# Rewriting the first batch of a fused attention and mixer kernel: casts and squares on another engine, the first rsqrt earlier, and a later mixing schedule

## Chip, cores, metric

The kernel runs on one core of one Trainium2 chip. The metric is device microseconds of one execution; lower is better. Most numbers below are medians of several executions. "Granted clock" is the share of the full TensorE clock that the chip allowed on average over an execution.

## The reference

Eight batches of 12 heads, 448 positions and head width 64 go through attention with RMS-normalised queries and keys, and then through a mixer: a rank-32 mix over positions, and a two-layer network over 768 channels with 3072 hidden ones.

```python
q_n, k_n = rmsnorm(q, g_q), rmsnorm(k, g_k)        # x / sqrt(mean(x*x) + 1e-6) * g
attn = softmax(q_n @ k_n.T / sqrt(64)) @ v         # per head
x = attn with heads side by side                   # (8, 448, 768)
u = x + (x.T @ U @ V).T                            # U: 448 x 32, V: 32 x 448
out = u + relu(u @ w_ch1) @ w_ch2                  # 768 -> 3072 -> 768
```

## The kernel before

The program is recorded in a fixed order, and each engine is given its own instructions in that order; the timelines below show them starting in it. In steady state the attention of the next batch is woven into the two-layer network of the current one. Batch 0 has nothing to be woven into: its attention runs alone, and this part (the "head", about 46 us) is what the change rewrites.

A group ("t") is 4 heads; a pair ("p") is 2 heads, so batch 0 has groups 0 to 2 and pairs 0 to 5. Each pair has four exponentials of 112 x 896, so the head has 24 "slots", numbered 0 to 23. In each slot one exponential is issued on ScalarE, then the pieces listed for that slot, then the score multiply of two slots later.

```python
def squares(t, hs=ALL, ss=(0, 1), eng=None):      # s=0: keys, s=1: queries
    ...
        if (t < 2 or t > 5) and eng is None:
            nc.scalar.activation(sqs[t, s][:, hs], qks[t, s][:, hs], AF.Square)
        else:
            nc.gpsimd.tensor_tensor(sqs[t, s][:, hs], qks[t, s][:, hs], qks[t, s][:, hs], OP.mult)
def reduce(t, hs, ss): ...       # VectorE: sums of the squares -> rstd
def rsqrt(t, hs): ...            # ScalarE: Ln, then Exp(-0.5 x), on rstd
def scale(t, pr): ...            # VectorE: qkn = qk * rstd, two tensor_tensor with two SBUF inputs
def transposes(p): ...           # TensorE, then two VectorE copies into qkT
def yield_port(t, pr):           # GpSimd waits here until that scale is done
    nc.gpsimd.tensor_copy(scratch, qkns[2 * t + pr][0:1, 1, 0, 0, 0:1])
def values(p, hh): ...           # TensorE: o = E^T va; VectorE: reciprocal, x, xs
def mix_a(b, dc): ...            # TensorE: pm = x_cols * U; VectorE: t4b <- pm
def mix_b(b, dc):                # TensorE: pu = t4b * V + x_cols
    ...
        if dc in (0, 5):
            nc.scalar.activation(us[b][:, dc, :], pu, AF.Copy)
        else:
            nc.vector.tensor_copy(us[b][:, dc, :], pu)
def heat(n): ...                 # n filler multiplies of 128 x 512, meant to keep TensorE's clock up
def first(i, dcs, start): ...    # first-layer multiplies of hidden blocks 2i and 2i+1
```

The order of the head, cut to what is argued about:

```python
heat(NWARM)                                  # NWARM = 16
squares(0, A); reduce(0, A)                  # A: first two heads of group 0, Bh: the others
nc.vector.tensor_mul(grow[:, 0], grow[:, 0], grow[:, 1])
squares(0, Bh, (0,)); rsqrt(0, A); squares(0, Bh, (1,))
reduce(0, Bh, (0,)); scale(0, 0); gain(); reduce(0, Bh, (1,))
transposes(0); heat(3)
squares(1, ALL, (0,), nc.gpsimd)
rsqrt(0, Bh)
scores(0, (0, 1))
at(0, scale, 0, 1)  ...  at(0, transposes, 1)
at(1, squares, 1, ALL, (1,))  ...  at(1, squares, 2)          # the first on ScalarE, the second on GpSimd
at(3, rsqrt, 1); at(3, scale, 1, 0)  ...
at(5, transposes, 2); at(5, scale, 1, 1)  ...
at(11, setup_v); at(11, rsqrt, 2); at(11, scale, 2, 0)
at(12, mix_a, 0, 0)
...
at(22, values, 4, 1); at(22, mix_a, 0, 3)
at(23, mix_b, 0, 3);  at(23, mix_a, 0, 4)
# after slot 23
first(0, range(0, 3), True)
values(5, 0); values(5, 1); mix_b(0, 4)
first(0, (3,), False); first(1, range(0, 4), True)
mix_a(0, 5); first(0, (4,), False); first(1, (4,), False); mix_b(0, 5)
...
```

The softmax here doesn't subtract the row's maximum and nothing guards it: scores larger than these inputs give would overflow.

Of the kernel before, what the change touches and what calls it, by code (L numbers as in the profile page):

```python
# [12 lines left out]
AF = mybir.ActivationFunctionType  # L13
# [4 lines left out]
def kernel(  # L18
# [13 lines left out]
    nc = tc.nc  # L32
# [7 lines left out]
    NJ = 4  # L40
# [43 lines left out]
    V4 = consts.tile([P, S], BF16, name="V4")  # L84
# [2 lines left out]
    grow = consts.tile([1, 2, 2, D], FP32, name="grow")  # L87
    one = consts.tile([1, 1], FP32, name="one")
    eps = consts.tile([SP, 1], FP32, name="eps")
    NWARM, NH = 16, 2  # L90
    FA, FM, NPE, FA0 = (0.74, 0.77), 0.09, 14, 0.66
    flat = Tw.rearrange("p f c n -> p (f c n)")
    lent = [0]
# [43 lines left out]
    def gain():  # L137

        pg = ps_mm.tile([P, 1], FP32, tag="mm")
        nc.tensor.matmul(pg, grow[:, 0].rearrange("o a d -> o (a d)"), one, start=True, stop=True)  # L140
        nc.vector.tensor_copy(gg, pg)
# [4 lines left out]
    Vf = lend(P, [S], FP32)  # L146
# [5 lines left out]
        nc.sync.dma_start(Vf, moe_V.rearrange("r s -> () r s").to_broadcast([4, rank, S]))  # L152

    def setup_v():
        nc.scalar.activation(V4.rearrange("r (j p) -> r j p", j=NJ), Vf.rearrange("r (p j) -> r j p", j=NJ), AF.Copy)
        nc.gpsimd.tensor_copy(Vsh[:, 0, 0:64], V4[:, 384:448])
        nc.gpsimd.tensor_copy(Vsh[:, 1, 64:128], V4[:, 0:64])

# [56 lines left out]
    ALL = slice(0, HG)  # L215

    def squares(t, hs=ALL, ss=(0, 1), eng=None):
        for s in ss:
            if (t, s) not in sqs:

                sqs[t, s] = early[0:SP, t, s] if t < 4 else norm.tile([SP, HG, NJ * D], FP32, tag="sq", name="sq", bufs=1)
# [5 lines that stand above are left out]
    def reduce(t, hs=ALL, ss=(0, 1)):  # L227
        if t not in rstds:
            rstds[t] = norm.tile([SP, 2, HG, NJ], FP32, tag="rstd", name="rstd", bufs=3)
        for s in ss:  # L230
            nc.vector.tensor_reduce(rstds[t][:, s, hs].rearrange("p h j -> p (h j)"),  # L231
                                    sqs[t, s][:, hs].rearrange("p h (j d) -> p (h j) d", d=D), AX, OP.add)

    def rsqrt(t, hs=ALL):
        rs = rstds[t][:, :, hs].rearrange("p s h j -> p s (h j)")
        nc.scalar.activation(rs, rs, AF.Ln, bias=eps)
        nc.scalar.activation(rs, rs, AF.Exp, scale=-0.5)  # L237

    def scale(t, pr):
        rstd, qkn = rstds[t], norm.tile([SP, 2, NJ, 2, D], BF16, tag="qkn", name="qkn")  # L240
        qkns[2 * t + pr] = qkn
        hp = slice(2 * pr, 2 * pr + 2)
        for s in range(2):
            nc.vector.tensor_tensor(  # L244
                qkn[:, s].rearrange("p j h d -> p h j d"),
                qks[t, s][:, hp].rearrange("p h (j d) -> p h j d", d=D),
                rstd[:, s, hp].rearrange("p h j -> p h j ()").to_broadcast([SP, 2, NJ, D]),
                OP.mult)

    def transposes(p):  # L250
        qkn = qkns[p].rearrange("p s j h d -> p (s j) (h d)")
        qkT = attn.tile([P, 2, S], BF16, tag="qkT")
        qkTs[p] = qkT
        if p < NPE:
            pt = ps_mm.tile([P, 2, S], BF16, tag="mm")
            for i in range(2 * NJ):
                nc.tensor.transpose(pt.rearrange("d s (j p) -> d (s j) p", j=NJ)[:, i, :], qkn[:, i, :], ident[:SP, :SP])
            nc.vector.tensor_scalar(qkT[:, 1], pt[:, 1], gg, None, OP.mult)
            nc.vector.tensor_copy(qkT[:, 0], pt[:, 0])
        else:  # L260
            nc.sync.dma_start_transpose(qkT.rearrange("d s (j p) -> d (s j) p", j=NJ), qkn)

# [97 lines left out]
    def mix_b(b, dc):  # L360

        xt, cs = x_tiles(b), slice(dc * P, (dc + 1) * P)
        pu = ps_mm.tile([P, 384], FP32, tag="mm")
        nc.tensor.matmul(pu, t4s[b][:, cs], V4[:, 0:384], start=True, stop=False)
        for i in range(3):
            nc.tensor.matmul(pu[:, i * P:(i + 1) * P], xt[i][:, cs], ident, start=False, stop=(i == 2))
        if dc in (0, 5):
            nc.scalar.activation(us[b][:, dc, :], pu, AF.Copy)
        else:
            nc.vector.tensor_copy(us[b][:, dc, :], pu)  # L370
# [145 lines left out]
    def attention(b, extra={}):  # L516
# [14 lines left out]
        for p in range(b * 6, b * 6 + 6):  # L531
# [32 lines left out]
            if p + 1 < NPE and odd:  # L564
                add(.5, transposes, p + 1)
# [25 lines left out]
    def head():  # L591

        A, Bh = slice(0, 2), slice(2, 4)
        load(0, 2)
        load(1)
        load(2)
        load_mix()
        load_v(0)
        load_v(1)
        load_v(2)  # L600
        load(3)
        load_v(3)
        setup()
        heat(NWARM)
        squares(0, A)
        reduce(0, A)
        nc.vector.tensor_mul(grow[:, 0], grow[:, 0], grow[:, 1])
        squares(0, Bh, (0,))
        rsqrt(0, A)
        squares(0, Bh, (1,))  # L610
        reduce(0, Bh, (0,))
        scale(0, 0)
        gain()
        reduce(0, Bh, (1,))
        transposes(0)
        heat(3)
        squares(1, ALL, (0,), nc.gpsimd)
        rsqrt(0, Bh)
        scores(0, (0, 1))
        fill = {n: [] for n in range(24)}  # L620

        def at(n, fn, *args):
            fill[n].append(lambda: fn(*args))

        at(0, scale, 0, 1)
        at(0, reduce, 1, ALL, (0,))
        at(0, heat, 3)
        at(0, transposes, 1)
        at(1, heat, 3)
        at(1, squares, 1, ALL, (1,))  # L630
        at(1, reduce, 1, ALL, (1,))
        at(1, yield_port, 0, 1)
        at(1, squares, 2)
        at(1, load_w1, 0)
        at(2, heat, 2)
        at(3, rsqrt, 1)
        at(3, scale, 1, 0)
        at(3, yield_port, 1, 0)
        at(3, nc.gpsimd.tensor_copy, Uc, Uf)
        at(3, cast_v, 0)  # L640
        at(3, heat, NH)
        at(4, heat, 2)
        at(5, heat, 1)
        at(6, heat, 1)
        at(5, transposes, 2)
        at(5, scale, 1, 1)
        at(5, yield_port, 1, 1)
        at(6, cast_v, 1)
        at(6, load_w1, 1)
        at(7, setup_u, 0)  # L650
        at(7, reduce, 2, ALL, (0,))
        at(8, transposes, 3)
        at(8, reduce, 2, ALL, (1,))
        at(8, cast_v, 2)
        at(9, setup_u, 1)
        at(9, heat, 1)
        at(10, values, 0, 0)
        at(11, values, 0, 1)
        at(11, setup_v)
        at(11, rsqrt, 2)  # L660
        at(11, scale, 2, 0)
        at(12, mix_a, 0, 0)
        at(12, heat, 1)
        at(13, transposes, 4)
        at(13, scale, 2, 1)
        at(13, load, 4)
        at(13, load_v, 4)
        at(13, load_w1, 2)
        at(14, values, 1, 0)
        at(14, yield_port, 2, 1)  # L670
        at(14, squares, 3)
        at(15, values, 1, 1)
        at(16, transposes, 5)
        at(16, load, 5)
        at(16, load_v, 5)
        at(16, load_w1, 3)
        at(16, cast_v, 3)
        at(16, mix_b, 0, 0)
        at(17, values, 2, 0)
        at(18, values, 2, 1)  # L680
        at(18, mix_a, 0, 1)
        at(19, values, 3, 0)
        at(19, mix_b, 0, 1)
        at(20, values, 3, 1)
        at(20, mix_a, 0, 2)
        at(21, values, 4, 0)
        at(21, mix_b, 0, 2)
        at(22, values, 4, 1)
        at(22, mix_a, 0, 3)
        at(23, mix_b, 0, 3)  # L690
        at(23, mix_a, 0, 4)
        for n in range(24):
            expo(*divmod(n, 4))
            for piece in fill[n]:
                piece()
            if n + 2 < 24:
                scores((n + 2) // 4, ((n + 2) % 4,))
        first(0, range(0, 3), True)
        values(5, 0)
        values(5, 1)  # L700
        mix_b(0, 4)
        first(0, (3,), False)
        first(1, range(0, 4), True)
        mix_a(0, 5)
        first(0, (4,), False)
        first(1, (4,), False)
        mix_b(0, 5)
        reduce(3)
        rsqrt(3)
        first(0, (5,), False)  # L710
        first(1, (5,), False)
        scale(3, 0)
        scale(3, 1)
        squares(4, ALL, (0,))
# [40 lines left out]
    def heat(n):  # L755
        if n:
            warm = ps_mm.tile([P, 512], FP32, tag="mm")
            for _ in range(n):
                nc.tensor.matmul(warm, xss[1][:, 0:P], xss[1][:, 0:512], start=True, stop=True)  # L759
# [46 lines left out]
```

## Time and profile before

| | before |
|---|---|
| median of the first 3 executions | 580.83 us (579.06 to 581.6) |
| median with 3 more, taken beside the changed kernel | 579.7 us (578.13 to 581.6) |
| profiled execution | 578.24 us, span 576.5 us, granted clock 1.0 |

From the page of the profile of before: the first line is the span, then each engine's busy time with its share of the span, then TensorE's busy tenths and its granted clock in 40 equal slices.

```profile
span 576.5 us, 11342 instructions
PE 559.5 (97%) x4590; PEld 305.9 (53%) x4613; DVE 395.5 (69%) x811; ACT 280.1 (49%) x413; POOL 77.4 (13%) x122
PE   7899999999999999999999999999999999999997
PEclk9999999999999999999999999999999999999999
```

TensorE (PE) is busy 97% of the span. Only 17 us are not, and over half of them lie in the first 46 us. The next view is busy time by stretch of the same execution; the columns are the stretch, its length, the busy time and count of TensorE, weight loads, VectorE, ScalarE and GpSimd, then the granted clock, the DMA share and GB/s.

```profile
0.00:11.68 11.68, 7.51 (x33) 2.98 (x33) 5.32 (x11) 4.69 (x9) 5.82 (x22) 1.00 0.81 198
11.68:28.50 16.82, 14.20 (x146) 7.08 (x147) 15.32 (x30) 16.13 (x22) 10.78 (x15) 1.00 1.14 233
28.50:37.73 9.23, 8.58 (x158) 6.08 (x156) 7.44 (x31) 7.42 (x9) 5.43 (x6) 1.00 1.16 244
37.73:45.60 7.87, 6.65 (x77) 4.35 (x77) 5.27 (x15) 0.49 (x1) 2.98 (x3) 1.00 1.12 236
100.00:576.00 476.00, 469.22 (x3659) 253.85 (x3678) 316.70 (x632) 219.17 (x323) 37.75 (x62) 1.00 0.42 96
```

From 11.68 to 28.5 us ScalarE is busy 16.1 of 16.8 us and VectorE 15.3: these two pace the front. From 28.5 us on TensorE paces, and after 100 us it has almost no gaps. Here is the timeline of ScalarE in the front (start, length, engine, line, operation, tiles; in brackets the idle time before it and what ended it):

```profile
6.73 0.63 ACT L223 ACTIVATE w2b<-qk 112x512 f32<-112x512 f32 x1 [1.47 <-DMA qk<-in_k_dram]
7.26 0.29 ACT L236 ACTIVATE rstd<-rstd,eps 112x16 f32<-112x16 f32 x1
...
10.60 0.31 ACT L236 ACTIVATE rstd<-rstd,eps 112x16 f32<-112x16 f32 x1 [2.21 <-DVE rstd L231]
...
11.68 1.73 ACT L278 ACTIVATE E<-sc 112x896 bf16<-112x896 f32 x2 [0.53 <-PE sc L273]
13.29 1.06 ACT L223 ACTIVATE w2b<-Tw 112x1024 f32<-112x1024 f32 x1
14.24 1.73 ACT L278 ACTIVATE E<-sc 112x896 bf16<-112x896 f32 x2
15.83 0.34 ACT L236 ACTIVATE rstd<-rstd,eps 112x32 f32<-112x32 f32 x1
```

The first rsqrt (7.26 us) stands behind squares that wait for a load, although its sum was ready at about 6.0 us. The "end of the head" is here and below the first multiply of tile `ph`, where the rest of the first layer begins; 24 multiplies of that layer are done earlier by `first`, among the mixing, from 38.98 us on. Between the last exponential (36.80 us) and the end of the head (45.60 us) TensorE has two waits:

```profile
engine line waited for: us in total, times, longest us
PE pu L364 <- DVE t4b L358: 0.8, 1, 0.8
PE first L732 <- ACT u L368: 0.6, 1, 0.6
```

The 0.8 us is `mix_b(0, 3)` in slot 23: it waits for the VectorE copy of `mix_a(0, 3)` issued just before it.

### The profile page before, as it was taken

The page shows a single profiled execution, that of the slowest core. Times are in us where ns is not written, and L with a number is a line of the kernel's source. Part 1 is how long each engine was busy: PE and PEld are TensorE (multiplying, and loading weights), DVE is VectorE, ACT ScalarE, POOL GpSimd, SP SyncE. Part 2 cuts the span into 40 slices and gives each one's busy share as a digit, 9 for nine tenths or more (in the row PEclk, how much of TensorE's full clock was granted, in tenths as well). Part 3 has the DMA queues.
Part 4 walks back from the last instruction along what each step waited for, and adds up shares of the span by engine and source line. Part 5 has one row for each costly group of instructions (what it writes and reads, how often), then busy time and mean ns, then how long its engine had stood idle before and what let it go on. Part 6 is the DMA issues. An engine that isn't in the chain of part 4 may idle for free.

```text
span 576.5 us, 11342 instructions
## 1 busy us (share of the span) xinstructions
PE 559.5 (97%) x4590; PEld 305.9 (53%) x4613; DVE 395.5 (69%) x811; ACT 280.1 (49%) x413; POOL 77.4 (13%) x122
## 2 busy tenths in 40 slices
PE   7899999999999999999999999999999999999997
PEld 2465556544565555544465555544456555554464
DVE  5878987399875787657776598747767487453442
ACT  5957661266622775166641776246661475302200
POOL 4743411000020000001020000000001000000010
PEclk9999999999999999999999999999999999999999
DMA  8999998434644555445535455456334541040021
GB/s 205 234 241 238 239 173 174 115 76 70 122 127 107 123 127 133 103 92 113 129 82 110 106 128 123 120 136 129 76 75 132 127 97 34 29 110 0 1 56 55
DMA packets 103648, 67.22 MB, mean 117 GB/s; under 512 B 54716, under 2 KB 102060, under 8 KB 103596
## 3 DMA queue, kind: packets, MB, share of 16 engines
q1 hardware_dynamic: 93988, 56.77, 42.5%
q0 software_dynamic: 9376, 9.44, 9.9%
q8 instruction: 36, 0.59, 0.4%
q10 hardware_dynamic: 232, 0.30, 0.2%
q14 instruction: 16, 0.13, 0.1%
HBM read 52.19 MB, written 11.01 MB: 110 GB/s over the span
## 4 chain that ended last, share of the span: by engine, by line
PE 85%; DVE 5%; DMA 4%; ACT 2%; SPq 1%; issue 1%; POOL 1%; DVEq 0%; POOLq 0%
PE ph L488 34%; PE pb L413 11%; PE po L413 8%; PE pe L413 7%; PE o L299 7%; PE pa L413 7%; PE sc L273 7%; DMA Tw<-in_v_dram 3%; PE pu L337 2%; ACT E L278 2%; DVE qkn L244 1%; SPq L198 1%; DMA qkT<-qkn 1%; PE warm L759 1%; DVE rstd L231 1%
## 5 line engine op out<-in xcount | busy, mean ns | idle before, releaser
L488 PE MATMUL ph<-u,w1b 128*128 128x384 bf16 (+1 forms) x1107 | 231.0, 353 | 1.4 <-DMA u<-x 0.2
L278 ACT ACTIVATE E<-sc 112x896 bf16<-112x896 f32 x184 | 160.0, 915 | 57.5 <-PE sc L273 56.4
L488 PEld LDWEIGHTS <-w1b 128*128 128x128 bf16 x1128 | 102.9, 98 | 108.4 <-issue 22.6
L413 PEld LDWEIGHTS <-hT 128*128 128x128 bf16 x1080 | 101.3, 98 | 71.5 <-issue 9.2
L491 ACT ACTIVATE hT<-ph 128x384 bf16<-128x384 f32 (+1 forms) x95 | 51.5, 543 | 135.9 <-PE ph L488 133.8
L493 DVE TENSOR_SCALAR hT<-ph 128x512 bf16<-128x512 f32 (+1 forms) x93 | 57.9, 622 | 53.9 <-PE ph L488 53.2
L299 PEld LDWEIGHTS <-E 112*128 112x128 bf16 x1472 | 58.6, 98 | 16.1 <-DVE xs L306 1.6
L299 PE MATMUL o<-va,E 112*128 112x65 bf16 x1440 | 60.9, 194 | 0.8 <-DVE xs L306 0.5
L244 DVE TENSOR_TENSOR qkn<-qk,rstd 112x512 bf16<-112x512 f32 x84 | 55.4, 697 | 7.8 <-ACT rstd L237 4.0
L273 PE MATMUL sc<-qkT 64*128 64x448 bf16 x384 | 55.5, 355 | 3.4 <-ACT E L278 1.3
L413 PE MATMUL po<-w2b,hT 128*128 128x384 bf16 x288 | 52.5, 326 | 0.6 <-DVE hT L493 0.6
L231 DVE TENSOR_REDUCE rstd<-sq 112x16 f32<-112x1024 f32 x40 | 48.5, 1212 | 4.8 <-ACT sq L223 4.1
L720 POOL COPY scratch<-qkn 1x1 bf16<-1x1 bf16 x44 | 10.3, 235 | 305.5 <-DVE qkn L244 305.0
L413 PE MATMUL pa<-w2b,hT 128*128 128x384 bf16 x264 | 49.5, 326 | 0.0
L413 PE MATMUL pb<-Tw,hT 128*128 128x384 bf16 x264 | 48.0, 326 | 0.0
L223 ACT ACTIVATE sq<-qk 112x1024 f32<-112x1024 f32 x36 | 38.3, 1063 | 2.3 <-issue 1.1
L303 DVE TENSOR_TENSOR x<-o,rec 128x192 bf16<-128x192 f32 x96 | 34.3, 357 | 3.7
L448 POOL TENSOR_TENSOR o<-o,x 128x384 f32<-128x384 f32 x11 | 12.6, 1145 | 161.2 <-DVE o L447 161.2
L302 DVE RECIPROCAL rec<-o 128x4 f32<-128x4 f32 x96 | 17.0, 177 | 23.6 <-PE o L299 23.2
L273 PEld LDWEIGHTS <-qkT 64*128 64x128 bf16 x384 | 12.5, 94 | 34.9 <-issue 30.9
L428 ACT ACTIVATE pb<-pa 128x384 f32<-128x384 f32 x11 | 5.2, 475 | 50.1 <-PE pa L413 50.1
L339 DVE TENSOR_TENSOR x<-pu,x 128x768 bf16<-128x768 f32 (+1 forms) x27 | 23.3, 865 | 7.2 <-PE pu L337 7.0
(106 smaller groups left out, 448.4 us busy)
## 6 DMA issues: line engine op xcount, KB each, us to landing
qk<-in_k_dram SPq DMA_DIRECT2D x21, 448.0 KB, 5.3
vt<-in_v_dram SPq DMA_DIRECT2D x20, 448.0 KB, 4.7
qk<-in_q_dram SPq DMA_DIRECT2D x19, 448.0 KB, 4.0
w2b<-in_moe_w_ch_dram POOLq DMA_DIRECT2D x6, 768.0 KB, 14.0
w1b<-in_moe_w_ch_dram POOLq DMA_DIRECT2D x2, 1536.0 KB, 21.0
out_dram<-o SPq DMA_DIRECT2D x15, 168.0 KB, 2.5
out_dram<-o SPq DMA_DIRECT2D x16, 144.0 KB, 2.1
out_dram<-o SPq DMA_DIRECT2D x15, 120.0 KB, 2.1
```

The costliest lines, as they stand in the source:

```text
L223: nc.scalar.activation(sqs[t, s][:, hs], qks[t, s][:, hs], AF.Square)
L231: nc.vector.tensor_reduce(rstds[t][:, s, hs].rearrange("p h j -> p (h j)"), sqs[t, s][:, hs].rearrange("p h (j d) -> p (h j) d", d=D), AX, ...
L244: nc.vector.tensor_tensor(qkn[:, s].rearrange("p j h d -> p h j d"), qks[t, s][:, hp].rearrange("p h (j d) -> p h j d", d=D), rstd[:, s, h ...
L273: nc.tensor.matmul(sc[:, hh, 0:S], kT[pp, kc * SP:kc * SP + P], qT[pp, :], start=True, stop=True)
L278: nc.scalar.activation(E_of(p)[:, :, PAD + kc * S:PAD + (kc + 1) * S], scs.pop((p, kc))[0:SP, :, 0:S], AF.Exp, scale=float(D) ** 0.5)
L299: nc.tensor.matmul(o[:, i, :], E[:, hh, c:c + P], va[:, hl, kc, :], start=(kc == 0), stop=(kc == NJ - 1))
L303: nc.vector.tensor_tensor(x3[:, :, d0:d0 + D], o[:, t0:t0 + 3, 0:D], rec[:, t0:t0 + 3].rearrange("p c -> p c ()").to_broadcast([P, 3, D]), ...
L339: nc.vector.tensor_add(xv, pu[rows, 0:n, 0:HALF], xv)
L413: nc.tensor.matmul(ps, lhs[:, c, :], rhs[:, c, :], start=first and c == 0, stop=last and c == NC - 1, skip_group_check=again)
L488: nc.tensor.matmul(ph, w1b[:, dc, hc * P:(hc + 1) * P], u[:, dc, :], start=(dc == 0), stop=(dc == KD - 1))
L491: nc.scalar.activation(hT[:, hc, 0:n], ph, AF.Relu)
L493: nc.vector.tensor_relu(hT[:, hc, 0:n], ph)
```

## The change

Its intent is to take work off ScalarE in the front, to start the first rsqrt earlier, and to give TensorE mixing pieces whose operands are already there. The diff, with small moves of `heat`, `yield_port` and `cast_v` cut:

```diff
-    NWARM, NH = 16, 2
+    NWARM, NH = 13, 2
     def setup_v():
-        nc.scalar.activation(V4..., Vf..., AF.Copy)
+        nc.gpsimd.tensor_copy(V4..., Vf...)
     # transposes(p): key copy of pair 0
-            nc.vector.tensor_copy(qkT[:, 0], pt[:, 0])
+            on VectorE if p else on ScalarE
     # mix_b
-        if dc in (0, 5):
+        if dc == 5:                            # first u copy on VectorE
     # head
         squares(0, A); reduce(0, A)
-        tensor_mul(grow...)
-        squares(0, Bh, (0,)); rsqrt(0, A); squares(0, Bh, (1,))
-        reduce(0, Bh, (0,)); scale(0, 0); gain(); reduce(0, Bh, (1,))
-        transposes(0); heat(3)
+        rsqrt(0, A); squares(0, Bh); scale(0, 0)
+        tensor_mul(grow...); gain(); reduce(0, Bh, (0,))
+        transposes(0); heat(2)
         squares(1, ALL, (0,), nc.gpsimd)
-        rsqrt(0, Bh)
         scores(0, (0, 1))
+        reduce(0, Bh, (1,))
+        at(0, rsqrt, 0, Bh)                    # now behind exponential 0
+        at(0, squares, 1, ALL, (1,), nc.gpsimd)
-        at(1, squares, 1, ALL, (1,))           # was on ScalarE
-        at(1, squares, 2)
+        at(1, squares, 2, ALL, (0,))
+        at(3, squares, 2, ALL, (1,))
-        at(11, setup_v)
+        at(6, setup_v)
-        at(12, mix_a, 0, 0)
+        at(14, mix_a, 0, 0)
-        at(17, values, 2, 0)
-        at(18, values, 2, 1); at(18, mix_a, 0, 1)
-        ...
-        at(22, values, 4, 1); at(22, mix_a, 0, 3)
-        at(23, mix_b, 0, 3);  at(23, mix_a, 0, 4)
+        for q in range(2, 5):
+            at(13 + 2 * q, values, q, 0); at(13 + 2 * q, mix_a, 0, q - 1)
+            at(14 + 2 * q, values, q, 1); at(14 + 2 * q, mix_b, 0, q - 1)
         # after slot 23
-        first(0, range(0, 3), True)
         values(5, 0)
+        mix_a(0, 4)
+        first(0, range(0, 4), True)
         values(5, 1)
         mix_b(0, 4)
-        first(0, (3,), False)
         first(1, range(0, 4), True)
```

More of the change, by code (lines that the diff above doesn't have):

```diff
@@ L154, in setup_v @@
     def setup_v():
-        nc.scalar.activation(V4.rearrange("r (j p) -> r j p", j=NJ), Vf.rearrange("r (p j) -> r j p", j=NJ), AF.Copy)
+        nc.gpsimd.tensor_copy(V4.rearrange("r (j p) -> r j p", j=NJ), Vf.rearrange("r (p j) -> r j p", j=NJ))
         nc.gpsimd.tensor_copy(Vsh[:, 0, 0:64], V4[:, 384:448])
@@ L258, in transposes @@
             nc.vector.tensor_scalar(qkT[:, 1], pt[:, 1], gg, None, OP.mult)
-            nc.vector.tensor_copy(qkT[:, 0], pt[:, 0])
+            if p:
+                nc.vector.tensor_copy(qkT[:, 0], pt[:, 0])
+            else:
+                nc.scalar.activation(qkT[:, 0], pt[:, 0], AF.Copy)
         else:
@@ L606, in head @@
         reduce(0, A)
+        rsqrt(0, A)
+        squares(0, Bh)
+        scale(0, 0)
         nc.vector.tensor_mul(grow[:, 0], grow[:, 0], grow[:, 1])
-        squares(0, Bh, (0,))
-        rsqrt(0, A)
-        squares(0, Bh, (1,))
+        gain()
         reduce(0, Bh, (0,))
-        scale(0, 0)
-        gain()
+        transposes(0)
+        heat(2)
+        squares(1, ALL, (0,), nc.gpsimd)
+        scores(0, (0, 1))
         reduce(0, Bh, (1,))
-        transposes(0)
-        heat(3)
-        squares(1, ALL, (0,), nc.gpsimd)
-        rsqrt(0, Bh)
-        scores(0, (0, 1))
         fill = {n: [] for n in range(24)}
@@ L623, in at @@
             fill[n].append(lambda: fn(*args))
+        at(0, rsqrt, 0, Bh)
         at(0, scale, 0, 1)
+        at(0, yield_port, 0, 1)
+        at(0, squares, 1, ALL, (1,), nc.gpsimd)
         at(0, reduce, 1, ALL, (0,))
@@ L629, in head @@
         at(1, heat, 3)
-        at(1, squares, 1, ALL, (1,))
         at(1, reduce, 1, ALL, (1,))
-        at(1, yield_port, 0, 1)
-        at(1, squares, 2)
+        at(1, squares, 2, ALL, (0,))
         at(1, load_w1, 0)
@@ L638, in head @@
         at(3, yield_port, 1, 0)
+        at(3, squares, 2, ALL, (1,))
         at(3, nc.gpsimd.tensor_copy, Uc, Uf)
-        at(3, cast_v, 0)
         at(3, heat, NH)
@@ L643, in head @@
         at(5, heat, 1)
-        at(6, heat, 1)
         at(5, transposes, 2)
@@ L647, in head @@
         at(5, yield_port, 1, 1)
-        at(6, cast_v, 1)
+        at(5, cast_v, 0)
+        at(6, heat, 1)
+        at(6, setup_v)
         at(6, load_w1, 1)
@@ L653, in head @@
         at(8, reduce, 2, ALL, (1,))
-        at(8, cast_v, 2)
+        at(8, cast_v, 1)
         at(9, setup_u, 1)
@@ L658, in head @@
         at(11, values, 0, 1)
-        at(11, setup_v)
         at(11, rsqrt, 2)
         at(11, scale, 2, 0)
-        at(12, mix_a, 0, 0)
-        at(12, heat, 1)
+        at(12, heat, 2)
+        at(12, yield_port, 2, 0)
+        at(12, cast_v, 2)
         at(13, transposes, 4)
@@ L673, in head @@
         at(16, transposes, 5)
+        at(16, mix_b, 0, 0)
         at(16, load, 5)
@@ L677, in head @@
         at(16, cast_v, 3)
-        at(16, mix_b, 0, 0)
-        at(17, values, 2, 0)
-        at(18, values, 2, 1)
-        at(18, mix_a, 0, 1)
-        at(19, values, 3, 0)
-        at(19, mix_b, 0, 1)
-        at(20, values, 3, 1)
-        at(20, mix_a, 0, 2)
-        at(21, values, 4, 0)
-        at(21, mix_b, 0, 2)
-        at(22, values, 4, 1)
-        at(22, mix_a, 0, 3)
-        at(23, mix_b, 0, 3)
-        at(23, mix_a, 0, 4)
+        for q in range(2, 5):
+            at(13 + 2 * q, values, q, 0)
+            at(13 + 2 * q, mix_a, 0, q - 1)
+            at(14 + 2 * q, values, q, 1)
+            at(14 + 2 * q, mix_b, 0, q - 1)
         for n in range(24):
```

## The prediction

> **What bounds the kernel now.** The page shows TensorE busy 559.5 us of a 576.5 us span, at granted clock 1.0. The change touches only batch 0, about the first 46 us; by stretch, TensorE is busy 469.2 of 476 us after 100 us. In the head:
> - 0 to 11.68 us (first exponential): warm-up multiplies run to about 9.46 us, ten at the slow rate (about 0.43 us) and six at 0.21. ScalarE's first rsqrt, whose sum was ready at about 6.0 us, stands behind squares that wait for a load until 6.73 us, and starts at 7.26.
> - 11.68 to 28.5 us (exponentials 0 to 15): ScalarE busy 16.1 of 16.8 us, VectorE 15.3. The chain of waits alternates.
> - 28.5 to 45.6 us: TensorE sets the pace (8.6 of 9.2 us, then 6.7 of 7.9 while ScalarE is nearly idle), with gaps for mixing operands: 0.82 us at 38.4, 0.58 at 44.9.
>
> **What the change does.** From ScalarE go one squares (1.06 us), the V cast (1.03) and one u copy (0.49); a key copy of 0.38 to 0.5 us comes to it from VectorE. GpSimd gets the squares at 1.89 us and the V cast (estimated 0.7, from its 1024-wide cast at 1.04). VectorE gets the u copy (0.54) and loses the key copy (0.38).
>
> **Worth, step by step.**
> 1. First rsqrt at about 6.0 instead of 7.26 us, three warm-ups fewer (-0.64 us): the warm-up's end is again the gate; first exponential at about 10.9 us, 0.7 to 0.9 earlier.
> 2. That lead is lost. The second rsqrt now follows exponential 0, so the second scale starts about 1 us later. Query squares of the second head group finish on GpSimd only at about 15.6 us (14.35 on ScalarE before), their sum near 16.8; the third rsqrt then starts about 1 us later than the old 15.96, and exponential 4 at about 17.4 (before 16.34). ScalarE waits about 1 to 2 us here.
> 3. A DVE scale meeting a GpSimd square stretches from 0.68 to 1.53 or 1.07 us in this trace, which agrees with the Trainium skill, "GPSIMD Engine Reference", section 1, that GpSimd contends for SBUF interfaces with VectorE instructions of two SBUF inputs. One such meeting goes (the scale at 16.47); one comes (third squares beside the scale near 21).
> 4. So around exponentials 8 to 15 the head is level with before to 1 us behind; the ScalarE time removed becomes idle, because VectorE's sums and scales release it.
> 5. The first mixing no longer waits on fresh values (0.79 us at 25.5), and the last mixing pieces are spread, so most of the 0.82 us gap and part of the tail's 1.6 us go. This is the gain that lasts: about 1 to 1.5 us at the end of the head.
>
> By both orders and the trace's durations, I estimate the end of the head 0.4 to 1.2 us earlier. Later stages are TensorE-bound and should pass it on, unless the saturated loads (DMA share above 1 until 80 us) take some back.
>
> **Prediction: 579.5 us**, range 577.0 to 582.0; faster by over 2%: 0.01, within 2%: 0.98, slower: 0.01.
>
> **What would show it.** First exponential near 10.9 us; exponential 4 later than 16.34, ScalarE waiting for VectorE's sum before it; exponential 16 within 1 us of 29.0; TensorE waiting less on the mixing copies from 37 to 46 us; the first layer after the head (18 multiplies from 45.6 us) starting at 44.4 to 45.3; unchanged stages after 100 us.
>
> **What would make it wrong.** The sum chain costing more than the mixing regains (slower by 1 us); GpSimd's fuller queue delaying weight loads or casts (several us); fewer warm-ups letting the clock fall; or the squares on GpSimd not gating at all (2 to 3 us faster).

## The result

| | before | changed |
|---|---|---|
| median of 6 | 579.7 us (578.13 to 581.6) | 580.0 us (579.82 to 581.03) |
| ratio, 95% interval | | 1.0006 (0.9985 to 1.0028) |
| profiled execution | 578.24 us, clock 1.0 | 581.03 us, clock 0.994 |

A ratio is the mean time of one kernel's executions over that of the other's of the same rounds, so it is not quite the ratio of the medians. The change neither gained nor lost anything that these executions can tell from noise. The profiled execution of the changed kernel is the slowest of its six, so what it shows has to be compared with care. From its page:

```profile
span 579.2 us, 11337 instructions
PE 561.7 (97%) x4587; PEld 306.2 (53%) x4610; DVE 396.5 (68%) x811; ACT 279.4 (48%) x411; POOL 79.6 (14%) x125
PE   5999999999999999999999999999999999999997
PEclk9799999999999999999999999999999999999999
```

The second slice of the granted clock has fallen: TensorE ran at half clock for a while in the head. By stretch, with the stretches set to the times at which the clock record changes (the third number from the end is the granted clock):

```profile
10.68:14.09 3.41, 1.57 (x12) 0.43 (x9) 1.72 (x3) 2.13 (x4) 1.90 (x1) 1.00 1.13 220
14.09:17.50 3.41, 3.41 (x13) 0.93 (x13) 2.94 (x4) 1.37 (x2) 3.41 (x3) 0.50 1.13 211
20.92:24.33 3.41, 2.46 (x28) 1.24 (x27) 3.41 (x6) 2.89 (x4) 2.13 (x4) 1.00 1.13 230
24.33:27.74 3.41, 3.41 (x38) 2.05 (x37) 2.96 (x8) 2.19 (x5) 3.35 (x6) 0.50 1.19 246
```

Each fall lasts 3.41 us and follows a stretch in which TensorE had gaps: it was busy 1.57 of 3.41 us, then 2.46. The first row beside ScalarE's timeline in the front of the changed kernel:

```profile
5.86 0.31 ACT L236 ACTIVATE rstd<-rstd,eps 112x16 f32<-112x16 f32 x1 [0.82 <-DVE rstd L231]
...
10.98 0.92 ACT L281 ACTIVATE E<-sc 112x896 bf16<-112x896 f32 x1 [0.46 <-PE sc L276]
11.79 0.30 ACT L236 ACTIVATE rstd<-rstd,eps 112x16 f32<-112x16 f32 x1
...
15.17 0.92 ACT L281 ACTIVATE E<-sc 112x896 bf16<-112x896 f32 x1 [2.03 <-PE sc L276]
17.05 0.92 ACT L281 ACTIVATE E<-sc 112x896 bf16<-112x896 f32 x1 [0.96 <-PE sc L276]
17.86 0.31 ACT L236 ACTIVATE rstd<-rstd,eps 112x32 f32<-112x32 f32 x1
```

The first rsqrt and the first exponential do come earlier (5.86 instead of 7.26, 10.98 instead of 11.68 us). But the second rsqrt is at 11.79 instead of 10.60, behind the exponential, and exponential 2 then waits 2.03 us, because TensorE's next score multiply stands behind transposes that need the second scale. The third rsqrt is 2 us later than before. The second scale in this profile, on VectorE, the GpSimd square beside it, and the transposes on TensorE that wait for it:

```profile
12.37 1.06 DVE L244 TENSOR_TENSOR qkn<-qk,rstd 112x512 bf16<-112x512 f32 x1 [1.84 <-ACT rstd L237]
10.99 1.90 POOL L225 TENSOR_TENSOR w2b<-qk 112x1024 f32<-112x1024 f32 x1 [6.43 <-DMA qk<-in_k_dram]
13.49 0.37 PE L257 MATMUL pt<-ident,qkn 112*128 112x112 bf16 x4 [1.61 <-DVE qkn L244]
```

This scale was stretched by the square (1.06 instead of 0.69 us) before the clock fell at 14.09. At the end of the head, TensorE's waits in the same stretch as shown of before (last exponential to the end of the head, 39.88 to 47.64 us):

```profile
PE first L728 <- ACT u L371: 0.6, 1, 0.6
```

The 0.8 us wait is gone. So the change gains at both ends and loses in between.

One profile is one execution, and the arrival of loads shifts its marks by some tenths. The time *between* marks is steadier. This table is worked out from the start times in the traces: the start of exponential 0, then the times from exponential 0 to 12, 12 to 16, 16 to 23, from 23 to the end of the head, from there to exponential 48 (the first of batch 2), and the half-clock time in the head. "Before, again" is a second profile of the same kernel; the other rows are the experiments below.

| kernel | exp 0 | 0-12 | 12-16 | 16-23 | 23-head end | head end to 48 | head end at | half clock |
|---|---|---|---|---|---|---|---|---|
| before | 11.68 | 13.22 | 4.11 | 7.79 | 8.79 | 65.90 | 45.60 | 0 |
| before, again | 12.05 | 12.57 | 4.10 | 7.80 | 8.79 | 65.89 | 45.31 | 0 |
| changed | 10.98 | 16.72 | 4.42 | 7.76 | 7.77 | 66.45 | 47.64 | 6.8 |
| mix_only | 12.21 | 13.86 | 4.75 | 8.36 | 7.77 | 66.32 | 46.95 | 3.4 |
| rs2_back | 11.49 | 14.39 | 4.45 | 7.77 | 7.77 | 65.89 | 45.87 | 0 |
| sq_back | 10.88 | 14.82 | 5.09 | 8.45 | 7.77 | 67.20 | 47.01 | 0 |
| heat_more | 11.84 | 15.25 | 4.45 | 7.76 | 7.77 | 67.07 | 47.07 | 0 |
| behind | 11.02 | 15.25 | 4.45 | 7.77 | 7.77 | 65.91 | 46.25 | 0 |
| combo | 11.23 | 14.32 | 4.27 | 7.78 | 7.77 | 67.46 | 45.36 | 0 |
| front_only | 11.51 | 13.44 | 4.89 | 8.35 | 8.79 | 67.01 | 46.98 | 3.4 |
| combo2 | 11.79 | 13.60 | 4.36 | 7.78 | 7.76 | 65.91 | 45.30 | 0 |
| tail_behind | 12.20 | 14.02 | 4.29 | 7.71 | 7.76 | 65.89 | 45.98 | 0 |
| tail_behind_heat | 11.53 | 15.48 | 4.56 | 7.71 | 7.77 | 65.90 | 47.04 | 0 |
| tail_only | 12.31 | 13.93 | 4.13 | 7.71 | 7.77 | 66.32 | 45.85 | 0 |

From exponential 48 to the end all rows lie between 464.7 and 465.4 us, so nothing after the second batch moved.

Not every stretch is steady. Five of these kernels have the order of before up to slot 11 (before, before again, mix_only, tail_behind, tail_only), and yet their 0-12 runs from 12.57 to 14.02 us, and exponential 12 starts between 24.62 and 26.24 us. It is shortest in "before, again", where no scale met GpSimd work, and long where two or three did (tail_only: scales of 1.12, 1.42 and 1.52 us instead of 0.69). So one profile's 0-12 of the old front is good to about 1.5 us only. A steadier mark is the time from exponential 0 to the third rsqrt, before most of these meetings: 4.15 to 4.46 us in those five and in front_only, 6.06 in behind and heat_more.

### The profile page after: what moved, and what is told of

The parts are those of the page before. It is cut to its first block, busy times and chain, and to the rows that moved or that the text cites. A ratio compares the mean times of both kernels' runs of the same rounds, so it can differ in the third digit from the quotient of the medians.

```text
span 579.2 us, 11337 instructions
## 1 busy us (share of the span) xinstructions
PE 561.7 (97%) x4587; PEld 306.2 (53%) x4610; DVE 396.5 (68%) x811; ACT 279.4 (48%) x411; POOL 79.6 (14%) x125
## 4 chain that ended last, share of the span: by engine, by line
PE 88%; DVE 6%; ACT 2%; DMA 2%; issue 1%; POOL 1%; DVEq 0%; POOLq 0%; ACTq 0%
PE ph L491 35%; PE pb L416 11%; PE po L416 8%; PE o L302 8%; PE pe L416 7%; PE sc L276 7%; PE pa L416 7%; DVE qkn L244 2%; PE pu L340 2%; ACT E L281 2%; PE warm L755 1%; DMA qkT<-qkn 1%; PE first L728 1%; PE pt L257 1%; DVE hT L407 1%
```

## The experiments

Theory 1: the change gains in the tail and loses in the front, through the second rsqrt behind exponential 0, the query squares on GpSimd and their collisions with VectorE. Theory 2: the fallen clock is what eats the gain. Rival to both: the mixing part gains nothing either, and the change is simply neutral.

### mix_only: the mixing part alone

On the kernel before, the lines of the change from `mix_b` and from slot 12 on, and nothing of the front:

```diff
-        if dc in (0, 5):
+        if dc == 5:
-        at(12, mix_a, 0, 0); at(12, heat, 1)
+        at(12, heat, 2)
+        at(14, mix_a, 0, 0)
-        (mixing pieces of slots 17 to 23, old tail)
+        (the loop over q, new tail)
```

> The kernel before with only the mixing part of the change (first mixing two slots later, the later mixing pieces and the tail rearranged, first u copy on VectorE). Theory 1 (the front of batch 0 loses what the mixing gains): exponential 0 to 8 as in before (11.7 and 20.3 us), the gap of 0.8 us before the fourth mixing's second half gone, first layer after the head starting 0.8 to 1.3 us earlier than the 45.6 us of before, total 0.8 to 1.3 us below before, granted clock 1.0 throughout. Rival (the mixing part gains nothing, the work is only moved inside a TensorE-bound stretch): start of that layer within 0.3 us of 45.6 and total within 0.4 us of before.

Median 579.66 us (578.05 to 581.15), ratio 0.9985 (0.996 to 1.0009): not clear of noise. The tail is 7.77 us instead of 8.79, as theory 1 has it. The head end was missed, by two things: exponential 12 came 1.2 us later than in before (26.08 us, with the front in before's order), and the profile has a half-clock fall from 29.5 to 32.9 us, which shows in 12-16 and 16-23. Its three executions at clock 0.999 or 1.0 took 578.05, 578.42 and 578.89 us, its other three 580.44 to 581.15.

### rs2_back: the second rsqrt ahead of exponential 0 again

```diff
+        reduce(0, Bh, (1,))
+        rsqrt(0, Bh)
         scores(0, (0, 1))
-        reduce(0, Bh, (1,))
...
-        at(0, rsqrt, 0, Bh)
```

> The changed kernel with only the second rsqrt (and the sum it needs) put back ahead of exponential 0. Theory 1 (the second rsqrt behind exponential 0 starts the late chain): second scale starts at 11.1 to 11.4 us instead of 12.37, exponential 2 at about 13 us instead of 15.17, exponential 4 still held to about 17 us by the query squares on GpSimd; head end 0.5 to 1 us earlier than in the changed kernel. Rival (the squares on GpSimd alone set the pace): exponential 4 and the head end within 0.3 us of the changed kernel.

Median 579.1 us, ratio 0.9982 (0.9959 to 1.0005). The second scale starts at 11.62 instead of 12.37 us (I had expected 11.1 to 11.4), exponential 2 at 14.09 instead of 15.17 (I had expected 13), exponential 4 at 17.18. Against the undisturbed head of the rewrite (row "behind"), 0-12 falls from 15.25 to 14.39, and all of it lies before the third rsqrt, which follows exponential 0 by 5.20 instead of 6.06 us: the late second rsqrt cost at least 0.9 us. In this execution the second scale met a GpSimd square (1.10 instead of 0.69 us), so without that about 1.3 is an estimate.

### sq_back: query squares of group 1 on ScalarE again

```diff
-        at(0, squares, 1, ALL, (1,), nc.gpsimd)
+        at(1, squares, 1, ALL, (1,))
```

> The changed kernel with only the query squares of the second head group back on ScalarE. Theory 1 (these squares on GpSimd gate the third rsqrt): third rsqrt starts at 16.2 to 17 us instead of 17.86, transposes of pair 2 0.8 us or more earlier, head end 0.5 to 1.2 us earlier than in the changed kernel. Rival (the second rsqrt sets the pace): less than 0.3 us changes anywhere.

Median 580.1 us, ratio 0.9996 (0.9972 to 1.002). The third rsqrt starts at 16.51 instead of 17.86 us in the changed kernel's profile, so these squares do gate it; but against the undisturbed head (17.08 in "behind") it is only 0.6 us, and 0-12 falls by 0.43 (15.25 to 14.82), as does the time from exponential 0 to the third rsqrt (6.06 to 5.63). In this execution the gain was lost again: two value casts on GpSimd met scales at 26.5 and 29.6 us (1.32 and 1.36 us instead of 0.69), and GpSimd waited 2.46 us for a load until 36.5 us.

### heat_more: more filler multiplies

On the changed kernel, 3 more multiplies in the warm-up and 16 more fillers:

```diff
-    NWARM, NH = 13, 2
+    NWARM, NH = 16, 2
-        transposes(0); heat(2)
+        transposes(0); heat(3)
-        at(0, heat, 3); at(1, heat, 3); at(2, heat, 2); at(5, heat, 1); at(6, heat, 1); at(9, heat, 1)
+        at(0, heat, 8); at(1, heat, 4); at(2, heat, 4); at(5, heat, 4); at(6, heat, 3); at(9, heat, 3)
```

> The changed kernel with 16 warm-up multiplies again and more filler multiplies in the gaps of the first ten slots. Theory of the clock (the profile of the changed kernel shows TensorE at half clock from 14.09 to 17.50 us and from 24.33 to 27.74 us, because its multiplies fill too little of the 3.4 us before): granted clock 1.0 from about 8 us on in every execution, the spread of its times at most 0.5 us, median 0.5 to 1.5 us below the changed kernel's 580.0 us though exponential 0 is up to 0.7 us later. Rival (the half clock hides in waits and costs nothing): head end not earlier than 47.8 us minus 0.3, median within 0.3 us of the changed kernel.

Half right. The clock is 0.999 or 1.0 in all six executions, as expected. But the median is 580.37 us, ratio 0.9996 (0.9975 to 1.0018): no gain. And the times spread over 2.1 us (579.26 to 581.33) instead of the 0.5 expected, so a steady clock alone does not make the time steady. Exponential 0 is 0.8 us later, and in the profile another loss appears after the head (67.07 us to exponential 48 instead of 65.90). That one is the next experiment.

### behind: one GpSimd square issued behind the scale

In batch 1 a GpSimd square waits for its load until about 59.5 us in most profiles. In the changed kernel's profile the head ends later, and a scale on VectorE meets it. VectorE, then GpSimd, in the changed kernel:

```profile
60.19 2.36 DVE L244 TENSOR_TENSOR qkn<-qk,rstd 112x512 bf16<-112x512 f32 x2
59.51 1.88 POOL L225 TENSOR_TENSOR sq<-qk 112x1024 f32<-112x1024 f32 x1 [0.18 <-DMA qk<-in_k_dram]
```

The same two in before, where the scale is just ahead:

```profile
58.14 1.29 DVE L244 TENSOR_TENSOR qkn<-qk,rstd 112x512 bf16<-112x512 f32 x2
59.38 1.88 POOL L225 TENSOR_TENSOR sq<-qk 112x1024 f32<-112x1024 f32 x1 [2.09 <-DMA qk<-in_k_dram]
```

Two scales take 1.29 us alone and 2.36 us beside the square. The edit issues that square after the `yield_port` that waits for the scale:

```diff
-            if odd and more2:
+            if odd and more2 and p != 7:
                 add(0, squares, t + 2, ALL, (0,))
...
                 add(0, yield_port, t + 1, 1)
+                if p == 7:
+                    add(0, squares, t + 2, ALL, (0,))
                 add(0, cast_v, t + 1)
```

> The changed kernel with one GpSimd square of batch 1 (the one that waits for a load until about 59.5 us) issued behind the scale on VectorE instead of beside it. Theory of the collision (in the changed kernel's profile the head ends 2 us later, so the scale meets that square at 60.19 us and takes 1.755 us instead of 0.69; in before it ended at 59.43, just ahead of it): no scale over 0.75 us between 45 and 112 us, 65.9 us from the first layer's start to exponential 48, as in before, instead of 66.5; total 0.4 to 1 us below the changed kernel's 580.0. Rival (the stretch hides in other waits): 66.4 us or more for that stretch.

As expected: 65.91 us from the head end to exponential 48, no stretched scale there, and in its profile:

```profile
58.80 1.29 DVE L244 TENSOR_TENSOR qkn<-qk,rstd 112x512 bf16<-112x512 f32 x2
60.23 0.18 POOL L718 COPY scratch<-qkn 1x1 bf16<-1x1 bf16 x1 [2.29 <-DVE qkn L244]
60.37 1.88 POOL L225 TENSOR_TENSOR sq<-qk 112x1024 f32<-112x1024 f32 x1
```

Median 579.64 us, ratio 0.998 (0.9956 to 1.0005). This kernel's head has exactly the changed kernel's order, so its profile at clock 1.0 is also the changed kernel's head without a fallen clock: 0-12 takes 15.25 us instead of 16.72. Of these 1.47 us, 0.37 is the second scale stretched before the first fall (12.37 us, above), so the two falls cost at most about 1.1 us in that execution. The totals of behind put it lower still for most: its executions at clock 1.0 took 579.11 to 579.55 us, those at 0.993 took 579.72 and 579.73, and one at 0.994 took 581.0.

### combo: the losing parts undone together

On the changed kernel, the edits of rs2_back, sq_back and behind together, and:

```diff
-        transposes(0); heat(2)
+        transposes(0); heat(3)
     def setup_v():
-        nc.gpsimd.tensor_copy(V4..., Vf...)
+        nc.scalar.activation(V4..., Vf..., AF.Copy)
-        at(6, setup_v)
+        at(11, setup_v)
```

> A version meant to beat both: the changed kernel with the second rsqrt ahead of exponential 0, the query squares and the V cast back on ScalarE, three filler multiplies after the first transposes, and the square of batch 1 behind the scale; the early first rsqrt, the mixing and the tail stay changed. Theory 1 (early rsqrt and mixing gain, the GpSimd work and the late second rsqrt lose): exponential 0 at about 11.2 to 11.6, exponential 4 at 16.4 or earlier, head end 44.4 to 45.3 us at full clock, median 577.8 to 578.8 us. Rival (the front is bound by loads and VectorE, whatever ScalarE holds): head end 45.5 us or later, median above 579.

Missed in the total: median 579.62 us (577.61 to 581.96), ratio 0.998 (0.9948 to 1.0013). The head ends at 45.36 us, at the edge of what was expected, and exponential 4 is at 16.66 us, later than expected. 0-12 is 14.32 us, hardly better than rs2_back alone. But here the second scale, at 11.36 us, met a GpSimd square and took 1.27 us; in combo2, which has the same order up to there, it took 0.69, and the third rsqrt follows exponential 0 by 4.36 instead of 4.95 us. Against 6.06 in behind that is 1.7 us, the sum of the two costs (0.43, and about 1.3 without the stretch), so up to the third rsqrt they do add up. This execution met another collision as well, a scale of 2.38 us at 46.93 (67.46 us to exponential 48).

### front_only: the first rsqrt alone

```diff
-        tensor_mul(grow...); squares(0, Bh, (0,)); rsqrt(0, A); squares(0, Bh, (1,))
-        reduce(0, Bh, (0,)); scale(0, 0); gain()
+        rsqrt(0, A); squares(0, Bh); scale(0, 0)
+        tensor_mul(grow...); gain(); reduce(0, Bh, (0,))
```

on the kernel before, with `NWARM` 13.

> The kernel before with only the first rsqrt ahead of the second half's squares, its scale earlier and 13 warm-up multiplies. Theory 1: exponential 0 at 10.9 to 11.2 us instead of 11.68, but the lead is gone by exponential 8, because the chain of sums on VectorE and squares on GpSimd is where it was: exponential 8 within 0.4 us of 20.3, time from exponential 23 to the head end 8.8 us as before, total within 0.5 us of before. Rival (the lead survives): exponential 8 at 19.6 us and total 0.7 us lower.

Median 580.39 us, ratio 0.9985 (0.9958 to 1.0012). Exponential 0 is at 11.51 us (expected 10.9 to 11.2), exponential 8 at 20.31 (before 20.28) and exponential 12 at 24.95 (before 24.90). So in this profile the lead is gone by exponential 8. It was small to begin with (0.17 us against the first profile of before, 0.54 against the second), and exponential 12 is within the spread of the old front, so this run alone shows no more. The clock fell in this execution too (27.6 to 31.0 us).

### before_again: a second profile of before

> The kernel before itself, profiled a second time, to see which marks of one profile repeat. Expected: the stretch from exponential 23 to the head end 8.8 us again (order alone sets it), while the arrival of loads, and with it exponential 0, moves by up to 0.5 us.

One execution, 577.77 us, state unknown. The tail is 8.79 us again, and exponential 0 moved by 0.37 us. From exponential 12 on the two profiles agree within 0.1 us in every stretch of the table. Without this run I would have taken the 0-12 of one profile (13.22, here 12.57) as firmer than it is.

### combo2: the third squares moved behind the scale

The rewrite splits the GpSimd squares of group 2; the second half then runs beside a scale. In combo, VectorE and then GpSimd:

```profile
19.40 1.64 DVE L244 TENSOR_TENSOR qkn<-qk,rstd 112x512 bf16<-112x512 f32 x1
18.37 1.88 POOL L225 TENSOR_TENSOR w2b<-hT 112x1024 f32<-112x1024 f32 x1
```

```diff
-        at(3, squares, 2, ALL, (1,))
...
         at(5, yield_port, 1, 1)
+        at(5, squares, 2, ALL, (1,))
```

> The combined version with the second half of the third squares moved behind the second scale of pair 3 on GpSimd. Theory of the collision (this scale took 1.53 to 1.64 us in each profile of the rewritten front at full clock, because that square runs beside it): no scale over 0.8 us near 19 to 21 us, exponential 0 to 12 in 13.4 to 14.0 us instead of 14.3. Rival: the time moves to the sum that waits for this square, and 0 to 12 stays at 14.2 or more.

In its profile, VectorE, GpSimd, and then the price on TensorE:

```profile
19.38 0.68 DVE L244 TENSOR_TENSOR qkn<-qk,rstd 112x512 bf16<-112x512 f32 x1
20.94 1.88 POOL L225 TENSOR_TENSOR w2b<-hT 112x1024 f32<-112x1024 f32 x1
23.87 0.67 PE L302 MATMUL o<-va,E 112*128 112x65 bf16 x16 [1.57 <-POOL va L213]
```

The collision is gone, and 0-12 falls to 13.60 us. Exponential 12 itself moves only from 25.55 to 25.39 us: the moved square delays the value cast behind it, and TensorE waits 1.57 us for that cast. Median 578.87 us (577.73 to 581.96), ratio 0.999 (0.996 to 1.0019).

### tail_behind, tail_behind_heat, tail_only: keep the tail and drop the rest

Since only the tail's gain was firm, the next versions start from the kernel before and take just the loop over q and the new tail (slot 17 onwards). `tail_behind` adds the square behind the scale; `tail_behind_heat` adds 15 fillers in slots 1 to 12 to that, with those of slot 12 ahead of the mixing; `tail_only` has neither. The edit of tail_only on the kernel before:

```diff
-        (values and mixing pieces of slots 17 to 23)
+        for q in range(2, 5):
+            at(13 + 2 * q, values, q, 0); at(13 + 2 * q, mix_a, 0, q - 1)
+            at(14 + 2 * q, values, q, 1); at(14 + 2 * q, mix_b, 0, q - 1)
-        first(0, range(0, 3), True)
         values(5, 0)
+        mix_a(0, 4)
+        first(0, range(0, 4), True)
         values(5, 1)
         mix_b(0, 4)
-        first(0, (3,), False)
         first(1, range(0, 4), True)
```

> The kernel before with only the last third of the change (mixing from slot 17 on and the tail after the last exponential), and the square of batch 1 behind the scale. Theory (the tail's 1.0 us is the part of the change that lasts, the front's parts give nothing): exponential 0 to 12 in 12.6 to 13.4 us, 12 to 16 in 4.1, 16 to 23 in 7.8, 23 to the head end in 7.8 us at full clock, head end 44.2 to 44.8 us, median 578.3 to 579.5 us with executions at half clock in between still 1 to 2 us longer. Rival (the mixing at the end needs the rest of the rewrite): 23 to the head end stays near 8.8 us or 16 to 23 grows by as much.

> The same with more filler multiplies in slots 1 to 12, where TensorE waits anyway. Theory of the clock (executions in which TensorE falls to half clock for 3.4 us in the head cost about 1.5 us each such fall): granted clock 0.999 or 1.0 in every execution, median 577.8 to 579.0 us, smaller spread than the 1.35 us of before; the fastest of all kernels. Rival (fillers take from the path what the clock gives): the median within 0.3 us of the version without fillers.

> The kernel before with only the mixing from slot 17 on and the tail changed; the square of batch 1 stays where it was. If the tail is what gains and the square behind the scale is a guard against a collision that only some executions have: 23 to the head end 7.8 us, median 577.6 to 579.0 us, and some executions (or the profile) with a scale over 1.5 us between 45 and 112 us. Rival (the gain of the version with both came from the square): median within 0.4 us of before.

| | median us | range | ratio to before | 95% interval |
|---|---|---|---|---|
| tail_only | 578.64 | 577.33 to 579.6 | 0.9963 | 0.9934 to 0.9992 |
| tail_behind | 577.68 | 576.95 to 578.86 | 0.9961 | 0.994 to 0.9983 |
| tail_behind_heat | 579.59 | 578.86 to 579.81 | 0.9989 | 0.9969 to 1.0009 |

The first two are the only versions whose interval excludes 1. Neither was timed beside the changed kernel; that they beat it follows only by way of before, with which the whole change is level (1.0006). In both the tail takes 7.76 to 7.77 us and 16-23 does not grow (7.71). They are 0.4% faster than before, some 2.2 us, which is more than the tail's 1.02 us. One of six executions of each had a fallen clock, against half of those of before, which would account for some of the rest. The executions bear this out: with those at clock 0.998 or more alone, five of each version against four and seven of before in the same rounds, the mean gain is 0.6 us for tail_only and 1.7 us for tail_behind, around the tail's 1.02. These are few executions, and why the clock fell less often was not tested. The median of tail_behind, expected at 578.3 to 579.5 us, came out lower (577.68). The head end, expected at 44.2 to 44.8 us for tail_behind, was missed (45.98): in this execution its front was slow, with exponential 0 at 12.20 us and scales of 1.40 and 2.04 us beside GpSimd squares at 11.7 and 17.3. The profile of tail_only has the expected collision after the head (a scale of 1.63 us at 58.39, 66.32 us to exponential 48), that of tail_behind has none. But the two were timed on different chips and their intervals overlap, so these runs do not show what the guard adds to the total.

`tail_behind_heat` is the clearest miss. All six executions are at clock 1.0 and their spread is the smallest of all (standard deviation 0.34 us, against 1.36 for the 44 executions of before), yet the median is 1.9 us above tail_behind on the same chip. Fillers buy a steady clock and here cost more than it is worth. In its profile the front is slow (0-12 15.48 us, scales of 1.75, 2.16 and 1.54 us beside GpSimd work), and some of its GpSimd work waits for loads. Which of its fillers lies on the path stays open.

### What the granted clock costs

This counts executions, and does not prove a cause. The kernel before was timed 44 times. In 22 of them the mean clock was 0.998 or more (mean 579.5 us); in 22 it was 0.997 or less (mean 581.4 us). One fall of 3.41 us to half is 0.003 of 578 us, and the values 0.997, 0.994, 0.991 and 0.987 are one to four of them. The changed kernel had falls in 3 of 6 executions (0.997, 0.994 and 0.993; mean 580.4 us, the others 580.0). Both kernels live with these falls. Theory 2 therefore explains a part of the slow profile, but not the missing gain: at 0.998 or more the changed kernel's three executions average 580.0 us against 579.5 for before.

## Why the prediction was right or wrong

The time was right: 579.5 predicted, range 577.0 to 582.0, measured 580.0. The direction inside it was not: a gain of about 1.3 us against the 580.83 us then known was predicted, and none came. That the number came out within 0.5 us is partly luck: the range also covers the kernel before, whose own executions went from 578.13 to 581.6 us.

- **First rsqrt and first exponential (step 1): right.** 5.86 and 10.98 us, predicted about 6.0 and 10.9.
- **The lead is lost (step 2): right in mechanism, and a little short in size.** Predicted: exponential 4 at about 17.4 and the third rsqrt about 1 us later. Measured with the clock undisturbed (behind): 17.57, and 17.08 instead of 15.83. Disturbed: 18.34 and 17.86. rs2_back and sq_back show both named causes, 0.9 and 0.4 us (0.9 in an execution with a stretched scale).
- **One collision goes and one comes (step 3): right.** The scale at 16.47 us (1.53 us) became 0.69; the one near 21 us took 1.53 us. The Trainium skill ("GPSIMD Engine Reference", section 1) names this contention, and these traces agree.
- **Exponentials 8 to 15 level to 1 us behind (step 4): the step that failed.** Exponential 12 was 2.8 us behind in the changed profile, and 1.4 us behind with the clock undisturbed (26.27 against 24.90); exponential 16, predicted within 1 us of 29.0, started at 32.12 and 30.71. The term was mis-sized: I let the losses overlap down to between zero and 1 us, while 0-12 took 15.25 us instead of 13.22 (12.57 to 14.02 in the five profiles of the old front, so that 1.2 to 2.7 us is what can be said). Undisturbed, exponential 8 was still 0.56 us behind (20.84 against 20.28), within the step; the other 0.8 us came between 8 and 12, where the collision of step 3 lies (the scale of 1.64 us at 20.30). In heat_more, where that scale took only 0.99 us, 8 to 12 took 4.63 us, as in before (4.62), instead of 5.43. That points to the collision, but is one profile.
- **Mixing and tail (step 5): right.** Predicted 1 to 1.5 us; the tail gives 1.02 us in every profile that has it. Of this, 0.82 us is the wait that vanished; the other 0.2 us is a mixing piece that went into an earlier stretch without lengthening it. But 12-16 took 0.34 us more, which I had not seen; its cause was not tested.
- **Head end 0.4 to 1.2 us earlier: wrong.** In the changed kernel's profile it is 2.0 us later. Undisturbed it is 0.65 to 0.94 us later (46.25 against 45.60 and 45.31). This last difference is smaller than the spread of the old front: tail_only and tail_behind, with that front and the new tail, end their heads at 45.85 and 45.98 us, so with the old tail's 1.02 us an old head may also end near 47 (an estimate). The sum, from the rows of the table: exponential 0 about 0.7 to 1.0 earlier, 0-12 2.0 to 2.7 later, 12-16 0.34 later, tail 1.02 earlier.
- **"Fewer warm-ups letting the clock fall"** was listed as what could go wrong, and the clock did fall in half of the executions. It fell as often in before, though. The Trainium skill ("TensorE: Matmul & The Clock Gate", part 1) describes a clock that is full or halved by how busy the array has been, judged over a free-running window of 3413 ns; the falls of 3.41 us agree.
- **After 100 us unchanged: right.** Between the head and there the collision at 60 us cost 0.55 us in the profiled execution, a stage I had taken to pass everything on.

The net of about +0.7 us at undisturbed clock is not resolved in the totals (interval of 1.3 us either way), so "no difference" is what the executions say. The sum above is how gains and losses can come to about nothing; the tail's gain and the two causes of the late third rsqrt are shown by runs of their own, the size of the net is not. The V cast on GpSimd, the key copy on ScalarE, the first u copy on VectorE and the moves of `cast_v` were not tested one by one.

## What to carry to other kernels

Taking work off an engine that was busy 96% of a stretch gained nothing here, because its items were released by other engines' chains (giving the squares back to it even shortened the chain by 0.4 us); follow the chain of the *last* released item, and test each moved piece alone, since a bundle of good and bad moves can come out as zero. Here the piece that lasted was giving the tensor engine operands that are a slot old (1.0 us), and taken alone it was 0.4% faster than before, with which the whole change is only level. Where an overlap costs as much as that of a scale and a GpSimd square (two scales of 1.29 us took 2.36), the two should be ordered by a dependency and not by luck: a later head or a later load brought them together. And before one profile's stretch is called a cost, compare it with profiles of kernels that have the same order there.

## What the Trainium skill lacked or had wrong

- "TensorE: Matmul & The Clock Gate", part 1: its rule is to avoid TensorE gaps longer than about 3.4 us. Here the clock fell to half at 14.09 us after a 3.41 us stretch whose longest gap was 1.61 us (TensorE busy 46%), and at 24.33 us after one whose longest gap was 0.54 us (busy 72%). The page tells of such falls from small gaps in its second failure mode, but gives no share of busy time to stay above; these runs give no clean threshold either: combo2 kept its full clock after 3.41 us (from 22.48) with TensorE busy 1.88 us, 55%.
- "GPSIMD Engine Reference", section 1: it names the contention with VectorE instructions of two SBUF inputs, but no size; another page, "SBUF — State Buffer", goes further, and section 1 does not point there. Measured here: a 112x512 `tensor_tensor` of 0.69 us took 0.99 to 2.38 us beside a 1.88 us GpSimd square, and ended 0.5 to 0.8 us after the square in the first 130 us of every trace, so it nearly waits the square out. VectorE sums with one SBUF input kept their 1.2 us beside the same squares.
- "GPSIMD Engine Reference", section 7: it puts reads at a stride of over 8 bytes at 50% more per element. The V cast on GpSimd (448 elements, read at a stride of 16 bytes) took 0.97 us, about as long as a contiguous cast of 1024 elements (1.03 us), so about twice as much per element (2.2 ns against 1.0); it was estimated at 0.7 us.
